# Softcapped attention and two feed-forward layers on one core: the column maxima put into PSUM, fewer and longer TensorE runs for the attention pairs, and a new placing of the planned steps

## The chip, the cores and the metric

One core of one Trainium2 chip runs the whole kernel. The metric is device time in microseconds of one execution. The engines are TensorE (PE; its weight loads are listed apart as PEld), VectorE (DVE), ScalarE (ACT), GpSimd (POOL) and SyncE (SP), which here only issues DMAs.

## The reference, cut to what matters

```
# q, k, v: (4 batches, 12 heads, 448 positions, 64), float32
scores = q @ k^T / sqrt(64)
scores = cap * tanh(scores / cap)
attn   = exp(scores - max over keys);  attn /= sum over keys + 1e-9
x      = attn @ v                     # heads side by side: (1792, 768)
h      = relu(x @ w_in)               # 768 -> 2048
x      = (h * h) @ w_out              # 2048 -> 768
g, val = x @ w_gate, x @ w_val        # 768 -> 1536 each
out    = (g * sigmoid(g) * val) @ w_out2   # 1536 -> 768
```

All is float32. The feed-forward matrices and their inputs are split into a high and a low float32r part, and each product is made of three matmuls (high by high, high by low, low by high).

## The kernel before, in words

**Attention pairs.** Two heads of a batch make a pair; six pairs a batch, 24 in all, numbered n = 6b + p. A pair goes through: load of k and q (`load_kq`) and of v; transposition to kT (batches 0 and 1: on TensorE by `tr_pe`, then two ScalarE copies by `tr_copy`; batches 2 and 3: on VectorE by `tr_v`); four blocks of 112 keys by 2 x 448 queries, each `scores` (TensorE, tile sc) and `tanh` (ScalarE, PSUM to SBUF, tile te or tt); `top`, three VectorE maxima over the four blocks (tile mx); `reduce`, a partition maximum on GpSimd (L250, tile mr); `sub`, four VectorE subtractions of mr (L256); `exp`, four on ScalarE (L260). Batches 0 and 1 then take `row_sum` and `av` on TensorE for each block; batches 2 and 3 add the four blocks first on VectorE (`total`, tile sm), then `total_sum` makes the sums and `av` weighs v, into two halves of one PSUM tile. `recip` is four steps on VectorE (a transpose L315 out of PSUM; small scalar steps L319 and L322; a reciprocal L326; a transpose L329), then `norm` (L334) and the split of the result by `x_hi` (ScalarE) and `x_lo` (VectorE, L348).

**Feed-forward units.** Pass 0 takes batches 0 and 1 with each weight piece, pass 1 batch 2, pass 2 batch 3. A unit is one output block of 128 by 448: six or four steps of three matmuls (`unit_mm`, L453, tile ff). In pass 0 each weight piece is loaded and rebuilt by three VectorE integer steps (`w_decode`, L418, L420, L422), stored to DRAM for the later passes, and split by `w_hi` (ScalarE) and `w_lo` (VectorE, L442). What leaves PSUM goes through ScalarE (relu, square, tanh) and VectorE (L480, L484, L492, L500).

**Order.** Nothing is ordered by hand. `Plan.order` places steps one by one: of all that could start, the one with the earliest start by the durations given to `plan.add`, and among equals the lowest rank (the fourth argument). The engines' instruction streams are then fixed in that order. The twelve pairs of batches 0 and 1 come ahead of nearly all feed-forward work (this stretch is called the attention stretch here); the pairs of batches 2 and 3 are strewn into passes 0 and 1, each opened by a unit named in `gates`, spaced by FIRST and LAST. `NPRE` = 3 weight pieces are used for batch 0 first, then for batch 1.

**PSUM**, eight banks: one score tile of two banks (tag s), a second (tag a: odd score blocks early, sums and weighed v later), four single banks (tag f) for everything else.

Of the kernel before, what the change touches and what calls it, by code (L numbers as in the profile page):

```python
# [20 lines left out]
class Plan:  # L21
# [15 lines left out]
    def order(self, free):  # L37
# [15 lines left out]
        blocked = {}  # L53
        dma = 0.0
        while len(seq) < len(ops):
            best = None
            for eng, some in ready.items():
                first = None
                for i in some:
                    _, _, _, rank, _, _, _, alloc, _ = ops[i]  # L60
                    t = max(since[i], free[eng])
                    for tag, bufs, _ in alloc:
                        old = rings.get(tag, ())
                        if len(old) >= bufs:
                            for d in old[-bufs]:
# [13 lines left out]
            if eng == "SP":  # L79
                free["SP"] = t + dur[0]  # L80
                dma = max(dma, t + 1.1) + dur[1]
                end[key] = dma + 1.1
            else:
                free[eng] = end[key] = t + dur
            seq.append((t, i))
# [11 lines left out]
def kernel(  # L97
# [33 lines left out]
    GB, TBUF, NPRE, NWARM = 10, 4, 3, 30  # L131
    FIRST = [17.0, 16.0]
    LAST = [60.0, 35.0]
# [7 lines left out]
    ps_f = ctx.enter_context(tc.tile_pool(name="ps_f", bufs=4, space=PSUM))  # L141

    V, A, G, PE = nc.vector, nc.scalar, nc.gpsimd, nc.tensor
    plan = Plan()
# [23 lines left out]

    def load_kq(b, p):
        d = pair[b, p] = {}  # L170
        if b < EARLY:
            n = ap.tile([CP, 2, NC, 2, D], F32, tag="kq", bufs=2, name="kq")
            for i, src in enumerate((k, q)):
                if (b, p) == (0, 0):
                    for j in range(2):
                        nc.sync.dma_start(n[:, i, :, j], src[b, j].rearrange("(p c) d -> p c d", c=NC))
                else:
                    nc.sync.dma_start(n[:, i], src[b, 2 * p : 2 * p + 2].rearrange("j (p c) d -> p c j d", c=NC))
        else:
            n = ap.tile([P, 2, TB, 32], F32, tag="kq", bufs=2, name="kq")  # L180
            for i, src in enumerate((k, q)):
                for g in range(4):
                    j, e = divmod(g, 2)
                    nc.sync.dma_start(
# [11 lines left out]
    def tr_pe(b, p, i):  # L196
        d = pair[b, p]
        pt = d["tr", i] = ps_f.tile([P, 512], F32, tag="f", name="tr")
        for c in range(NC):
            col = slice(c * CP, (c + 1) * CP) if i == 0 else slice(c, S, NC)  # L200
            PE.matmul(
                pt[:, col],
# [13 lines left out]
    def tr_copy(b, p, i):  # L216
        A.copy(kt(b, p)[:, i], pair[b, p].pop(("tr", i))[:, :S])
# [4 lines left out]
    def scores(b, p, c, tag):  # L222
        d = pair[b, p]
        pool = ps_s if tag == "s" else ps_a
        ps = d["s", c] = pool.tile([P, 2, 512], F32, tag=tag, name="sc")
        for j in range(2):
            r = slice(64 * j, 64 * j + 64)
            PE.matmul(  # L228
                ps[:CP, j, :S], d["kT"][r, 0, c * CP : (c + 1) * CP], d["kT"][r, 1], start=True, stop=True
            )  # L230

    def tanh(b, p, c):
        d = pair[b, p]
        if b < EARLY and c < 3:
            t = fp.tile([CP, 2, S], F32, tag="g", bufs=GB, name="te")
        else:
            t = ap.tile([CP, 2, S], F32, tag="t", bufs=TBUF, name="tt")
        d["t", c] = t
        A.activation(t, d.pop(("s", c))[:CP, :, :S], AF.Tanh, scale=c_inv)  # L239
# [7 lines left out]
    def reduce(b, p):  # L247
        d = pair[b, p]
        d["m"] = ap.tile([CP, 2, S], F32, tag="m", bufs=2, name="mr")
# [13 lines left out]
    def row_sum(b, p, c):  # L263
        d = pair[b, p]
        if c == 0:
            d["rs"] = ps_f.tile([P, 512], F32, tag="f", name="rs")
# [17 lines left out]
    def total_sum(b, p):  # L284
        d = pair[b, p]
        d["a"] = ps_a.tile([P, 2, 512], F32, tag="a", name="av")
        d["rs"] = d["a"][:, 1]
# [10 lines left out]
    def av(b, p, c):  # L298
        d = pair[b, p]
        if c == 0:  # L300
            d["av"] = ps_f.tile([P, 512], F32, tag="f", name="av") if b < EARLY else d["a"][:, 0]
        for j in range(2):
# [6 lines left out]
            )  # L309

# [134 lines left out]

    def unit_mm(ps, i, b, c):
# [3 lines left out]
        if c == 0:  # L450
            ffn_ps[i, b] = ps_f.tile([P, 512], F32, tag="f", name="ff")
# [50 lines left out]
    def out_tr(b, m):  # L502
        if m % 2 == 0:
            ob_t[b, m // 2] = fp.tile([P, TB, 2, 32], F32, tag="ob", bufs=2, name="ob")
# [20 lines left out]
    ACT1, ACT2, DVE1, DVE2 = 0.5, 0.98, 0.58, 1.04  # L525

    def plan_pair(n, at, gate=()):
        b, p = divmod(n, KD)
        early = b < EARLY
        pe = 0.0 if early else 0.8  # L530
        K = lambda name, *a: (name, n, *a)
        before = [("ld", n - 1)] if n else []
        add(K("ld"), "SP", (2.0, 1.4) if n == 0 else (1.3, 2.0) if early else (3.2, 1.5), at, load_kq, (b, p),
            before + list(gate), [("kq", 2, [K("tr", 0), K("tr", 1)])])
        add(K("lv"), "SP", (0.5, 0.7), at + 4, load_v, (b, p), [K("ld")], [("v", 2, [K("av", 3)])])
        for i in range(2):
            if early:
                add(K("tr", i), "PE", 0.56, at + 6, tr_pe, (b, p, i), [K("ld"), ("ident",)], [("f", 4, [K("cp", i)])])
                add(K("cp", i), "ACT", ACT1, at + 6, tr_copy, (b, p, i), [K("tr", i)],
                    [("kT", 2, [K("sc", 3)])] if i == 0 else [])  # L540
            else:
                add(K("tr", i), "DVE", DVE1, at + 6, tr_v, (b, p, i), [K("ld")],
                    [("kT", 2, [K("sc", 3)])] if i == 0 else [])
        src = K("cp", 1) if early else K("tr", 1)
        for c in range(NC):
            tag = "a" if early and c % 2 else "s"
            deps = [src, K("cp" if early else "tr", 0)] + ([K("sc", c - 1)] if c else [])
            add(K("sc", c), "PE", 0.78, at + 8 + c, scores, (b, p, c, tag), deps, [(tag, 1, [K("th", c)])], pe)
            tt = ("g", GB) if early and c < 3 else ("t", TBUF)
            add(K("th", c), "ACT", ACT2, at + 8.5 + c, tanh, (b, p, c), [K("sc", c)] + [("cap",)] * (n == 0),  # L550
                [(*tt, [K("av", c), K("rs", c) if early else K("tot", max(c, 1))])])
            if c:
                add(K("top", c), "DVE", DVE2, at + 9 + c, top, (b, p, c), [K("th", c), K("th", c - 1)] + [K("top", c - 1)] * (c > 1),
                    [("mx", 2, [K("par")])] if c == 1 else [])
        add(K("par"), "POOL", 3.2, at + 13, reduce, (b, p), [K("top", 3)], [("m", 2, [K("sub", 3)])])
        for c in range(NC):
            add(K("sub", c), "DVE", DVE2, at + 16 + c, sub, (b, p, c), [K("par")] + [K("sub", c - 1)] * (c > 0))
            add(K("ex", c), "ACT", ACT2, at + 17 + c, exp, (b, p, c), [K("sub", c)])
            if early:
                add(K("rs", c), "PE", 0.42, at + 18 + c, row_sum, (b, p, c), [K("ex", c)] + [K("rs", c - 1)] * (c > 0),  # L560
                    [("f", 4, [K("rc", 0)])] if c == 0 else [])
            elif c:
                add(K("tot", c), "DVE", DVE2, at + 19 + c, total, (b, p, c), [K("ex", c), K("ex", c - 1)],
                    [("mx", 2, [K("rs")])] if c == 1 else [])
        if not early:
            add(K("rs"), "PE", 0.5, at + 23, total_sum, (b, p), [K("tot", 3)], [("a", 1, [K("norm")])], pe)
        for c in range(NC):
            deps = [K("ex", c), K("lv")] + [K("av", c - 1)] * (c > 0) + [K("rs")] * (not early)
            add(K("av", c), "PE", 0.78, at + 19 + c, av, (b, p, c), deps,
                [("f", 4, [K("norm")])] if early and c == 0 else [], pe)  # L570
        for i, dur in enumerate((0.36, 0.7, 0.2, 0.62)):
            ring = {0: [("st", 1, [K("rc", 1)])], 1: [("rc", 2, [K("rc", 3)])], 3: [("rb", 1, [K("norm")])]}
            add(K("rc", i), "DVE", dur, at + 24 + i, recip, (b, p, i),
                [K("rc", i - 1)] if i else [K("rs", 3) if early else K("rs")], ring.get(i, ()))
        rel = [K("hold")] if b == 2 else [K("xl")]
        add(K("norm"), "DVE", DVE1, at + 28, norm, (b, p), [K("rc", 3), K("av", 3)], [("xs", 2, rel)])
        if b == 2:
            add(K("hold"), "SP", (0.4, 0.6), at + 30, hold, (p,), [K("norm")])
        else:
            s = lambda: x_t[b, p]  # L580
            add(K("xh"), "ACT", ACT1, at + 29, x_hi, (b, p, s), [K("norm")])
            add(K("xl"), "DVE", DVE1, at + 30, x_lo, (b, p, s), [K("xh")])
# [3 lines left out]
    PAIR = 7.6  # L586
# [27 lines left out]
    add(("ident",), "POOL", 8.0, -99, lambda: None)  # L614
    add(("cap",), "DVE", 0.8, -99, set_cap, (), [])
    for n in range(EARLY * KD):
        plan_pair(n, 10.6 * n)
    for i in range(NWARM):
        add(("warm", i), "PE", 0.43 if i < 8 else 0.22, 1e4 + i, warm, (i,), [("warm", i - 1)] if i else [],
            [("f", 4, [("warm", NWARM - 1)])] if i == 0 else [])  # L620
# [3 lines left out]
    for ps, (bs, seq) in enumerate(passes):  # L624
        for i in range(NB):
# [4 lines left out]
            if ps == 0:  # L630
                at = max(at - 14.0, 30.0 + 20 * i) if i < NPRE else at - 14.0
# [19 lines left out]
    for ps, (bs, seq) in enumerate(passes):  # L651
# [10 lines left out]
        for ps_, i, b, t in [s for s in steps if s[0] == ps]:  # L662
# [4 lines left out]
            for c in range(n):  # L667
# [103 lines left out]
```

## Time and profile before

| | |
|---|---|
| median of 3 runs | 1293.4 us (1288.98 to 1297.14) |
| the profiled execution | 1293.31 us, span 1291.3 us |
| busy share | PE 97%, PEld 77%, DVE 70%, ACT 44%, POOL 6% |
| chain that ended last | PE 83%, DVE 13%, ACT 1%, issue 1% |
| partition maxima | 24 on POOL, 77.9 us |
| feed-forward matmuls | 4896, 1020.9 us busy |

The profiled execution stands 0.1 us from the median and lies 2.0 us above its own span. A share of the whole span is a mean over two unlike stretches: the attention stretch, which lasts until about 179 us, and the feed-forward passes behind it. They are to be read apart.

### The profile page before, as it was taken

What the parts mean: (1) busy time and instruction counts of PE and PEld (TensorE: products, weight loads), DVE (VectorE), ACT (ScalarE), POOL (GpSimd) and SP (SyncE); (2) the same over time, 40 slices, a digit from 0 to 9 for tenths busy, and PEclk for the clock granted to TensorE, in tenths of its full rate; (3) what the DMA queues carried; (4) which work ended last, traced back from release to release, by engine and by line L of the source; (5) the groups of instructions that cost most, each with busy time, mean ns of one, the idle gap of its engine ahead of it and who ended that gap; (6) DMA issues with size and microseconds to landing.
All of it is one profiled execution on the core that took longest, in us unless ns stands there. A gap on an engine that the chain in (4) does not pass through costs nothing.

```text
span 1291.3 us, 16640 instructions
## 1 busy us (share of the span) xinstructions
PE 1246.6 (97%) x6300; PEld 996.8 (77%) x6300; DVE 906.4 (70%) x1341; ACT 568.6 (44%) x847; POOL 78.7 (6%) x31
## 2 busy tenths in 40 slices
PE   9887989999999999999999999999999999999997
PEld 5232457987986987987988987787787799999997
DVE  5999977668667867678778665777856843455454
ACT  6676644425344324323133375553453455433331
POOL 2232200000000000000000010000000000000000
PEclk9898989999998999999999999999999999999999
DMA  8331134664562572672664844254143353343323
GB/s 181 70 80 37 43 90 127 191 166 135 166 175 87 179 186 72 204 190 79 206 172 112 217 122 119 66 132 131 49 127 93 85 149 110 95 126 102 107 90 75
DMA packets 221983, 159.55 MB, mean 124 GB/s; under 512 B 143184, under 2 KB 190416, under 8 KB 221904
## 3 DMA queue, kind: packets, MB, share of 16 engines
q1 hardware_dynamic: 221904, 158.50, 43.8%
q8 instruction: 49, 0.80, 0.3%
q14 instruction: 30, 0.25, 0.1%
HBM read 124.85 MB, written 33.62 MB: 123 GB/s over the span
## 4 chain that ended last, share of the span: by engine, by line
PE 83%; DVE 13%; issue 1%; ACT 1%; SPq 0%; DMA 0%; DVEq 0%; ACTq 0%
PE ff L453 73%; PE av L303 4%; PE sc L228 4%; DVE mx L245 3%; DVE te L256 2%; DVE tt L256 1%; DVE rc L322 1%; DVE rc L319 1%; DVE sm L282 1%; PE warm L521 1%; DVE st L315 1%; PE rs L269 1%; DVE rb L329 1%; DVE wp L442 1%; DVE x L348 0%
## 5 line engine op out<-in xcount | busy, mean ns | idle before, releaser
L453 PE MATMUL ff<-x,wp 128*128 128x448 f32 x2880 | 600.9, 368 | 0.2 <-DVE x L348 0.2
L453 PEld LDWEIGHTS ff<-x,wp 128*128 128x128 f32 x2880 | 538.6, 188 | 71.9 <-issue 25.7
L453 PE MATMUL ff<-g,wp 128*128 128x448 f32 x2016 | 420.0, 367 | 0.1
L453 PEld LDWEIGHTS ff<-g,wp 128*128 128x128 f32 x2016 | 376.4, 188 | 48.9 <-issue 15.1
L437 ACT CAST wp<-wx 128x512 fp32r<-128x512 f32 (+1 forms) x246 | 176.9, 723 | 204.2 <-PE ff L453 141.4
L442 DVE TENSOR_TENSOR wp<-wx,wp 128x512 fp32r<-128x512 f32 (+1 forms) x246 | 206.8, 843 | 52.5 <-ACT wp L437 47.7
L492 DVE TENSOR_TENSOR g<-gg,g 128x448 fp32r<-128x448 f32 x112 | 69.9, 626 | 101.1 <-ACT g L488 101.0
L250 POOL PARTITION_ALL_REDUCE mr<-mx x24 | 77.9, 3247 | 926.3 <-DVE mx L245 926.3
L500 DVE TENSOR_TENSOR acc<-ff,acc 128x448 f32<-128x448 f32 x120 | 74.2, 621 | 48.7 <-PE ff L453 48.1
L228 PE MATMUL sc<-kT 64*112 64x448 f32 x384 | 93.7, 580 | 12.7 <-ACT te L239 10.9
L488 ACT CAST g<-gg 128x448 fp32r<-128x448 f32 x112 | 63.3, 565 | 71.6 <-DVE gg L484 69.7
L239 ACT ACTIVATE tt<-sc,capt 112x896 f32<-112x896 f32 x60 | 60.5, 1008 | 57.5 <-PE sc L228 57.3
L468 ACT ACTIVATE r<-ff 128x448 f32<-128x448 f32 x64 | 34.8, 544 | 91.3 <-PE ff L453 91.3
L476 ACT ACTIVATE th<-ff 128x448 f32<-128x448 f32 x48 | 26.2, 545 | 100.6 <-PE ff L453 100.6
L422 DVE SCALAR_TENSOR_TENSOR wx<-wr,wx 128x512 int32<-128x512 int32 (+1 forms) x82 | 68.4, 834 | 1.5
L420 DVE SCALAR_TENSOR_TENSOR wx<-wr,wx 128x512 int32<-128x512 int32 (+1 forms) x82 | 67.2, 820 | 2.1
L480 DVE SCALAR_TENSOR_TENSOR sg<-th,ff 128x448 f32<-128x448 f32 x48 | 29.6, 620 | 53.5 <-ACT th L476 53.3
L228 PEld LDWEIGHTS sc<-kT 64*112 64x112 f32 x384 | 27.9, 173 | 49.8 <-issue 22.7
L260 ACT ACTIVATE tt<-tt,capt 112x896 f32<-112x896 f32 x60 | 60.0, 1038 | 10.3 <-DVE tt L256 10.3
L303 PE MATMUL av<-tt,v 112*64 112x448 f32 x240 | 55.6, 576 | 7.8 <-DVE st L315 7.8
L256 DVE TENSOR_TENSOR tt<-tt,mr 112x896 f32<-112x896 f32 x60 | 62.1, 1084 | 1.1 <-POOL mr L250 1.1
L484 DVE SCALAR_TENSOR_TENSOR gg<-ff,sg 128x448 f32<-128x448 f32 x48 | 29.9, 623 | 33.8 <-PE ff L453 33.7
(54 smaller groups left out, 668.2 us busy)
## 6 DMA issues: line engine op xcount, KB each, us to landing
wx<-w SPq DMA_DIRECT2D x80, 384.0 KB, 3.1
wx<-w SPq DMA_DIRECT2D x84, 256.0 KB, 2.6
w<-wx SPq DMA_DIRECT2D x40, 384.0 KB, 2.7
wr<-in_moe_w_in_dram SPq DMA_DIRECT2D x16, 768.0 KB, 5.5
wr<-in_moe_w_out_dram SPq DMA_DIRECT2D x24, 512.0 KB, 4.0
w<-wx SPq DMA_DIRECT2D x42, 256.0 KB, 2.3
wr<-in_moe_w_gate_dram SPq DMA_DIRECT2D x12, 768.0 KB, 4.9
wr<-in_moe_w_val_dram SPq DMA_DIRECT2D x12, 768.0 KB, 4.9
```

Of the source, the lines that this page charges most:

```text
L228: PE.matmul(ps[:CP, j, :S], d["kT"][r, 0, c * CP : (c + 1) * CP], d["kT"][r, 1], start=True, stop=True)
L250: G.partition_all_reduce(d["m"].rearrange("p j s -> p (j s)"), d["mx"].rearrange("p j s -> p (j s)"), CP, bass_isa.ReduceOp.max)
L256: V.tensor_tensor(d["t", c], d["t", c], d["m"], ALU.subtract)
L303: PE.matmul(d["av"][64 * j : 64 * j + 64, :S], d["v"][:, j, c], d["t", c][:, j], start=(c == 0), stop=(c == NC - 1),)
L420: V.scalar_tensor_tensor(x, hi, -0x40000000, x, ALU.bitwise_and, ALU.bitwise_or)
L422: V.scalar_tensor_tensor(x, lo, 29, x, ALU.logical_shift_right, ALU.bitwise_or)
L437: A.copy(hl[:, 0], raws[ps, i])
L442: V.tensor_tensor(hl[:, 1], raws[ps, i], f32(hl[:, 0]), ALU.subtract)
L453: PE.matmul(ffn_ps[i, b][:, :S], hl[:, h, c], x[:, t], start=(c == 0 and s == 0), stop=(c == cnt(u) - 1 and s == 2),)
L488: A.copy(g_t[b, f][:, 0], tmp_t[i, b])
L492: V.tensor_tensor(g[:, 1], tmp_t.pop((i, b)), f32(g[:, 0]), ALU.subtract)
L500: V.tensor_tensor(acc, pt, acc, ALU.add)
```

## The change

- **Maxima in PSUM, for the twelve early pairs.** A new ScalarE step `top_copy` (planned as `mp`) copies mr into a PSUM tile (tag a); the four `sub` read it there. mr has one buffer in place of two. Late pairs' `sub` still read mr in SBUF.
- **Steps beside a partition maximum.** The planner is given a set `ports` of VectorE step names (top, xl, yl, wd, wl, rc, tot, gl). One whose start would lie within a planned partition maximum is planned at its end. No wait is added to the program by that.
- **Early PSUM.** The four f banks become two f0 and two f1. Early odd score blocks go into two f0 banks, one for each head, each with a tanh of its own; both transposes of a pair share one s tile and one ScalarE copy; sums and weighed v take f1.
- **The first pair** is loaded as the late ones are, k on SyncE's queue and q on ScalarE's, and transposed on VectorE.
- **Late pairs.** Two score blocks are one TensorE step into s and a, so two runs in place of four; `weigh` makes sums and all of `av` in one step, sums in a, weighed v in s.
- **Batch 1 begun ahead.** The first three units of batch 1 no longer wait for all its x and for the unit before them: each of their six steps needs only the x of one pair, and they may start once the last early tanh is done, in banks f0, f0 and s.
- **Placing.** All ranks, the planner's durations, and FIRST and LAST are new; the first pieces' rebuilding has ranks behind the early pairs; a fourth weight buffer (WP); the output tiles ob share the mx buffers.

```
-    def __init__(self):
+    def __init__(self, ports):
...
+                    if ops[i][0][0] in self.ports and pool[0] <= t < pool[1]:
+                        t = pool[1]
...
+    FIRST = [18.4, 16.8]
+    LAST = [66.8, 51.7]
+    DECODE = 138.4
...
+    def top_copy(b, p):
+        d = pair[b, p]
+        ps = ps_a.tile([P, 2, 512], F32, tag="a", name="mp")[:CP, :, :S]
+        A.copy(ps, d["m"])
+        d["m"] = ps
...
+    def weigh(b, p):
+        total_sum(b, p)
+        for c in range(NC):
+            av(b, p, c)
...
+        if halves(b, c):
+            ps = [ps_f.tile([P, 512], F32, tag="f0", name="sc")[:CP, :S] for _ in range(2)]
...
+                add(K("sc", c), "PE", 1.55, R("sc", c), lambda b, p, c: (scores(b, p, c), scores(b, p, c + 1)), (b, p, c),
+                    src + ([K("sc", c - 2)] if c else []), [("s", 1, [K("th", c)]), ("a", 1, [K("th", c + 1)])], pe)
...
+        if early:
+            add(K("mp"), "ACT", ACT2, R("mp"), top_copy, (b, p), [K("par")], [("a", 1, [K("sub", 3)])])
...
+                ahead = ps == 0 and b == 1 and i < NPRE
+                if c == 0 and u[0] == "1a" and not ahead:
...
+                if ahead and c == 0:
+                    deps.append((("th", EARLY * KD - 1, 3, 1), ("sub", EARLY * KD - 1, 3))[i == 3])
```

## Rows read from the trace of the kernel before

**Rows 1.** Busy time by windows: per engine us (instructions), then PEclk, DMA share, GB/s.
```profile
120.00:140.00 20.00, 17.50 (x131) 7.52 (x129) 19.37 (x31) 14.16 (x20) 2.86 (x1) 1.00 0.09 24
400.00:410.00 10.00, 7.31 (x26) 2.31 (x27) 7.69 (x17) 1.63 (x4) 0.00 (x0) 0.66 0.14 44
1100.00:1200.00 100.00, 100.00 (x496) 92.68 (x495) 52.88 (x76) 37.90 (x62) 0.00 (x0) 1.00 0.35 105
```

**Rows 2.** Groups of VectorE by form, 0 to 176 us.
```profile
L256 DVE TENSOR_TENSOR te<-te,mr 112x896 f32<-112x896 f32 x36 | 39.0, 1117 | 0.0
L322 DVE TENSOR_SCALAR rc<-st 32x7 f32<-32x7 f32 x46 | 15.3, 333 | 0.9
...
L319 DVE TENSOR_SCALAR rc<-st 128x14 f32<-128x14 f32 x12 | 9.8, 819 | 0.4
```

**Rows 3.** Timeline of VectorE in the attention stretch, and its last split.
```profile
14.96 1.09 DVE L245 TENSOR_TENSOR mx<-te 112x896 f32<-112x896 f32 x1 [10.77 <-ACT te L239]
...
19.50 2.57 DVE L245 TENSOR_TENSOR mx<-te 112x896 f32<-112x896 f32 x1
...
113.48 2.57 DVE L256 TENSOR_TENSOR te<-te,mr 112x896 f32<-112x896 f32 x1
...
116.41 0.17 DVE L319 TENSOR_SCALAR rc<-st 128x14 f32<-128x14 f32 x1
116.61 0.69 DVE L322 TENSOR_SCALAR rc<-st 32x7 f32<-32x7 f32 x4
...
178.82 0.61 DVE L348 TENSOR_TENSOR x<-xs,x 128x448 fp32r<-128x448 f32 x1
```

**Rows 4.** Timeline of GpSimd: one of the twelve early partition maxima, and a late one.
```profile
112.86 3.42 POOL L250 PARTITION_ALL_REDUCE mr<-mx  x1 [1.13 <-DVE mx L245]
...
815.15 2.86 POOL L250 PARTITION_ALL_REDUCE mr<-mx  x1 [44.73 <-DVE mx L245]
```

**Rows 5.** Timeline of VectorE beside the late one.
```profile
815.47 0.63 DVE L500 TENSOR_TENSOR acc<-ff,acc 128x448 f32<-128x448 f32 x1 [0.49 <-PE ff L453]
816.34 1.30 DVE L442 TENSOR_TENSOR wp<-wx,wp 128x768 fp32r<-128x768 f32 x1 [0.24 <-ACT wp L437]
```

**Rows 6.** Groups of ScalarE by form, 0 to 176 us.
```profile
L239 ACT ACTIVATE te<-sc,capt 112x896 f32<-112x896 f32 x36 | 34.9, 999 | 11.3 <-PE sc L228 11.2
```

**Rows 7.** Timeline of TensorE, attention stretch and just behind it.
```profile
10.33 1.70 PE L201 MATMUL tr<-ident,kq 112*128 112x112 f32 x16
...
131.80 1.76 PE L228 MATMUL sc<-kT 64*112 64x448 f32 x8
133.50 0.99 PE L201 MATMUL tr<-ident,kq 112*128 112x112 f32 x8
...
179.49 8.11 PE L453 MATMUL ff<-x,wp 128*128 128x448 f32 x38 [0.21 <-DVE x L348]
```

**Rows 8.** Chain of waits, one of the twelve late pairs: start, length, what.
```profile
219.98 69.01 PE ff L453 x333
288.99 0.94 PE sc L228 x4
289.93 2.01 PE ff L453 x9
...
314.80 0.52 PE av L290 x8
315.32 0.93 PE av L303 x4
...
316.83 2.48 PE av L303 x12
```

**Rows 9.** Waits of TensorE, 176 to 1291 us: total, times, longest.
```profile
PE av L303 <- DVE st L315: 7.8, 12, 1.1
PE av L290 <- DVE sm L282: 3.8, 2, 2.6
PE sc L228 <- DVE kT L220: 1.7, 1, 1.7
```

More of the change, by code (lines that the diff above doesn't have):

```diff
@@ L130 @@
     EARLY = 2
-    GB, TBUF, NPRE, NWARM = 10, 4, 3, 30
-    FIRST = [17.0, 16.0]
-    LAST = [60.0, 35.0]
+    GB, TBUF, WP, NPRE, NWARM = 10, 4, 4, 3, 30
+    FIRST = [18.4, 16.8]
+    LAST = [66.8, 51.7]
+    STRETCH = 2.91
+    AHEAD = dict(
+        ld=29.0, lv=13.4, tr=4.9, cp=4.1, sc=8.7, th=-4.3, top=-8.2, par=-0.6, mp=5.4, sub=29.5,
+        ex=22.2, rs=-1.8, av=30.4, rc=15.3, norm=-7.2, xh=27.4, xl=40.7,
+    )
+    LATER = dict(
+        ld=-14.4, lv=-4.9, tr=6.7, sc=-5.8, th=7.5, top=4.5, par=11.1, sub=28.9, ex=17.9,
+        tot=26.9, av=13.2, rc=1.5, norm=-0.6, xh=24.3, xl=36.9,
+    )
+    PACE = 6.97
+    SLACK = 2.11
+    MARGIN = 0.61
+    DECODE = 138.4
     const = ctx.enter_context(tc.tile_pool(name="const", bufs=1))
@@ L167, with rows @@
     x_t = {}
+    def rows(b, p):
+        return 0 < b * KD + p < EARLY * KD
     def load_kq(b, p):
         d = pair[b, p] = {}
-        if b < EARLY:
+        if rows(b, p):
             n = ap.tile([CP, 2, NC, 2, D], F32, tag="kq", bufs=2, name="kq")
             for i, src in enumerate((k, q)):
[L174 to L178, printed above, removed]
+                nc.sync.dma_start(n[:, i], src[b, 2 * p : 2 * p + 2].rearrange("j (p c) d -> p c j d", c=NC))
         else:
@@ L197, in tr_pe @@
         d = pair[b, p]
-        pt = d["tr", i] = ps_f.tile([P, 512], F32, tag="f", name="tr")
+        if i == 0:
+            d["tr"] = ps_s.tile([P, 2, 512], F32, tag="s", name="tr")
         for c in range(NC):
@@ L214, in kt, with tr_copy, halves, scores @@
         return d["kT"]
-    def tr_copy(b, p, i):
-        A.copy(kt(b, p)[:, i], pair[b, p].pop(("tr", i))[:, :S])
+    def tr_copy(b, p):
+        A.copy(kt(b, p), pair[b, p].pop("tr")[:, :, :S])
     def tr_v(b, p, i):
         V.transpose(out=kt(b, p)[:, i], in_=pair[b, p]["n"][:, i].rearrange("p t d -> p (t d)"))
-    def scores(b, p, c, tag):
+    def halves(b, c):
+        return b < EARLY and c % 2
+    def scores(b, p, c):
         d = pair[b, p]
-        pool = ps_s if tag == "s" else ps_a
-        ps = d["s", c] = pool.tile([P, 2, 512], F32, tag=tag, name="sc")
+        if halves(b, c):
+            ps = [ps_f.tile([P, 512], F32, tag="f0", name="sc")[:CP, :S] for _ in range(2)]
+        elif c % 2:
+            ps = ps_a.tile([P, 2, 512], F32, tag="a", name="sc")[:CP, :, :S]
+        else:
+            ps = ps_s.tile([P, 2, 512], F32, tag="s", name="sc")[:CP, :, :S]
+        d["s", c] = ps
         for j in range(2):
             r = slice(64 * j, 64 * j + 64)
[L228 to L232, printed above, removed]
+            to = ps[j] if halves(b, c) else ps[:, j]
+            PE.matmul(to, d["kT"][r, 0, c * CP : (c + 1) * CP], d["kT"][r, 1], start=True, stop=True)
+    def tanh(b, p, c, j=0):
         d = pair[b, p]
-        if b < EARLY and c < 3:
-            t = fp.tile([CP, 2, S], F32, tag="g", bufs=GB, name="te")
-        else:
-            t = ap.tile([CP, 2, S], F32, tag="t", bufs=TBUF, name="tt")
-        d["t", c] = t
-        A.activation(t, d.pop(("s", c))[:CP, :, :S], AF.Tanh, scale=c_inv)
+        if j == 0:
+            if b < EARLY and c < 3:
+                t = fp.tile([CP, 2, S], F32, tag="g", bufs=GB, name="te")
+            else:
+                t = ap.tile([CP, 2, S], F32, tag="t", bufs=TBUF, name="tt")
+            d["t", c] = t
+        if halves(b, c):
+            A.activation(d["t", c][:, j], d["s", c][j], AF.Tanh, scale=c_inv)
+        else:
+            A.activation(d["t", c], d.pop(("s", c)), AF.Tanh, scale=c_inv)
     def top(b, p, c):
@@ L248, in reduce @@
         d = pair[b, p]
-        d["m"] = ap.tile([CP, 2, S], F32, tag="m", bufs=2, name="mr")
+        d["m"] = ap.tile([CP, 2, S], F32, tag="m", name="mr")
         G.partition_all_reduce(
@@ L265, in row_sum @@
         if c == 0:
-            d["rs"] = ps_f.tile([P, 512], F32, tag="f", name="rs")
+            d["rs"] = ps_f.tile([P, 512], F32, tag="f1", name="rs")
         for g in range(4):
@@ L285, in total_sum @@
         d = pair[b, p]
-        d["a"] = ps_a.tile([P, 2, 512], F32, tag="a", name="av")
-        d["rs"] = d["a"][:, 1]
+        d["rs"] = ps_a.tile([P, 2, 512], F32, tag="a", name="rs")[:, 0]
         for g in range(4):
@@ L300, in av @@
         if c == 0:
-            d["av"] = ps_f.tile([P, 512], F32, tag="f", name="av") if b < EARLY else d["a"][:, 0]
+            if b < EARLY:
+                d["av"] = ps_f.tile([P, 512], F32, tag="f1", name="av")
+            else:
+                d["av"] = ps_s.tile([P, 2, 512], F32, tag="s", name="av")[:, 0]
         for j in range(2):
@@ L450, in unit_mm @@
         if c == 0:
-            ffn_ps[i, b] = ps_f.tile([P, 512], F32, tag="f", name="ff")
+            tag = f_tag(ps, i, b)
+            if tag in "sa":
+                ffn_ps[i, b] = (ps_s if tag == "s" else ps_a).tile([P, 2, 512], F32, tag=tag, name="ff")[:, 0]
+            else:
+                ffn_ps[i, b] = ps_f.tile([P, 512], F32, tag=tag, name="ff")
         for s, (h, t) in enumerate(((0, 0), (0, 1), (1, 0))):
@@ L555, in plan_pair @@
[L555 to L558, printed above, removed]
+        add(K("lv"), "SP", (0.5, 0.7), R("lv"), load_v, (b, p), [K("ld")], [("v", 2, [K("av", 3) if early else K("av")])])
+        tk = ("kT", 2, [K("sc", 3) if early else K("sc", 2)])
@@ new lines, in plan_pair @@
+        if rows(b, p):
+            for i in range(2):
+                add(K("tr", i), "PE", 0.42, R("tr"), tr_pe, (b, p, i), [K("ld"), ("ident",)] + [K("tr", 0)] * i + [("sc", n - 2, 3)] * (n > 1),
+                    [] if i else [("s", 1, [K("cp")])])
+            add(K("cp"), "ACT", ACT2, R("cp"), tr_copy, (b, p), [K("tr", 1)], [tk])
+            src = [K("cp")]
+        else:
+            for i in range(2):
+                add(K("tr", i), "DVE", 0.64, R("tr"), tr_v, (b, p, i), [K("ld")] + [K("tr", 0)] * i, [] if i else [tk])
+            src = [K("tr", 0), K("tr", 1)]
@@ new lines, in plan_pair @@
+        for c in range(NC):
+            half = halves(b, c)
+            ths = [K("th", c, 0), K("th", c, 1)] if half else [K("th", c)]
+            if early:
+                deps = src + ([K("sc", c - 1)] if c else [])
+                if c == 0 and n:
+                    deps.append(("sc", n - 1, 3))
+                add(K("sc", c), "PE", 0.84, R("sc", c), scores, (b, p, c), deps,
+                    [("f0", 2, [t]) for t in ths] if half else [("s", 1, ths)])
+            elif c % 2 == 0:
+                add(K("sc", c), "PE", 1.55, R("sc", c), lambda b, p, c: (scores(b, p, c), scores(b, p, c + 1)), (b, p, c),
+                    src + ([K("sc", c - 2)] if c else []), [("s", 1, [K("th", c)]), ("a", 1, [K("th", c + 1)])], pe)
+            tt = ("g", GB) if early and c < 3 else ("t", TBUF)
+            used = [K("av", c), K("rs", c)] if early else [K("av"), K("tot", max(c, 1))]
+            by = K("sc", c) if early else K("sc", c - c % 2)
+            for j, t in enumerate(ths):
+                add(t, "ACT", 0.51 if half else ACT2, R("th", c + 0.5 * j), tanh, (b, p, c, j),
+                    [by] + [("cap",)] * (n == 0) + ([ths[0]] if j else []), [] if j else [(*tt, used)])
+            if c:
+                prev = [K("th", 0)] if c == 1 else [K("top", c - 1)]
+                add(K("top", c), "DVE", DVE2, R("top", c), top, (b, p, c), ths + prev, [("mx", 2, [K("par")])] if c == 1 else [])
@@ L562, in plan_pair @@
             elif c:
-                add(K("tot", c), "DVE", DVE2, at + 19 + c, total, (b, p, c), [K("ex", c), K("ex", c - 1)],
-                    [("mx", 2, [K("rs")])] if c == 1 else [])
+                add(K("tot", c), "DVE", DVE2, R("tot", c), total, (b, p, c), [K("ex", c), K("ex", c - 1)],
+                    [("mx", 2, [K("av")])] if c == 1 else [])
         if not early:
[L566 to L570, printed above, removed]
@@ L586 @@
-    PAIR = 7.6
+            add(K("xh"), "ACT", ACT1, R("xh"), x_hi, (b, p, s), [K("norm")])
+            add(K("xl"), "DVE", DVE1, R("xl"), x_lo, (b, p, s), [K("xh")])
+    PAIR = 6.64
     steps = []
```

109 lines of the change are left out of this document (53 added, 56 removed).

## Prediction

> **What bounds the kernel now.** I read the windows first, because the page's shares mix two stretches. Up to about 179 us VectorE is the full engine: 19.37 of 20 us busy between 120 and 140, with TensorE at 17.50 and ScalarE at 14.16; in the feed-forward part it is TensorE, 100.00 of 100, with VectorE at 52.88 [rows 1]. So a microsecond taken from VectorE is worth something in the first stretch only, and one taken from TensorE in the second.
>
> The second view is VectorE's timeline. Its work starts in earnest at 14.96 and the last split of the attention stretch ends at 178.82 + 0.61 = 179.43 [rows 3]: 164.5 us, almost without idle time. But busy is not the same as working. The first step of `recip` (L319) takes 0.17 us when it starts behind the partition maximum, the four steps of L322 together 0.69 [rows 3], yet their means are 0.819 and 0.333 each [rows 2]. The excess is 12 x (0.819 - 0.17) = 7.8 us and 46 x (0.333 - 0.172) = 7.4 us. Four larger steps, the first at 19.50 and the last at 113.48, also have 2.3 to 2.6 us where a subtraction has 1.1 [rows 2, 3]: some 5.7 us together. Laid beside GpSimd's timeline, the step at 113.48 begins 0.6 us after a maximum does (112.86, 3.42 us) [rows 3, 4]. So about 21 us of VectorE's "busy" time is waiting beside twelve partition maxima, 1.7 us for each.
>
> The third view, the chain of waits, gives the price of a late pair on TensorE: four score runs of 0.94 us, each followed by nine feed-forward matmuls that take 2.01 where 69.01 / 333 x 9 = 1.87 would do, then sums 0.52, 0.93 for the first block of av, a hole, and 2.48 for the rest [rows 8]. The waits name the hole: the transpose L315 that reads the sums, 7.8 us over 12 pairs [rows 9].
>
> **The attention stretch.** Removing 21 us of collisions needs two things: the `sub` steps must not collide, and they must be what stands beside a maximum. For the first, the nearest rows are late ones. Beside the maximum at 815.15, L500, which reads one operand from PSUM, starts 0.32 us into it and takes 0.63; L442, with both operands in SBUF, starts 0.87 us later and takes 1.30 [rows 4, 5]; its 768 columns should take 0.95, an estimate between 0.61 for 448 columns and 1.09 for 896 [rows 3]. One row is thin, so I keep both ends: no gain from PSUM operands, or all of it. I take nearly all. [...] Four `sub` of 1.1 us are 4.4 us, longer than a maximum of 2.9 to 3.5 us [rows 2, 4], so a pair's `sub` can cover the next pair's maximum. But the engines' orders are fixed and nothing waits: a maximum that starts later or earlier than planned meets other steps again, and where no `sub` is ready VectorE idles instead. I take 17 of 21 us, with 21 and 6 as the ends.
>
> [...]
>
> What is added does not lie on VectorE. `top_copy` is one ScalarE step of some 1.0 us a pair by the tanh of the same size [rows 6]; halved odd tanhs add two starts a pair, some 0.2 us if a start costs there what 0.61 for 448 columns beside 1.09 for 896 shows on VectorE [rows 3]; one transposition copy in place of two gives 0.1 back. At 164.5 / 12 = 13.7 us a pair, ScalarE's 14.16 of 20 [rows 1] is 9.7 us a pair; it becomes 10.8, under the 12.3 that I expect VectorE to take. Without that slack the 13 us would lie on the path. The copy also lengthens the way from a maximum to its `sub` by 1.0 us and a handover, covered by the next pair's maxima and `recip` on VectorE. One buffer for mr is enough, as the copy empties it.
>
> **The start.** The first transposes on TensorE start at 10.33, then come a copy and the scores, and VectorE's first maximum is at 14.96 [rows 3, 7]. With kT made on VectorE, the scores can stand where the transposes stood, 1.6 us earlier; the warming matmuls ahead of them stay. Four DMA issues move to ScalarE's queue, which idles then. I take -1.5 (0 to -3).
>
> Together the stretch would end at 179.4 - 17 - 1.5 = 161. As a check, 164.5 us less the collisions is 143 us of VectorE work; from 13.4 that is 156 with no idle time, so my value leaves 5 us of idle time.
>
> **Batch 1 begun ahead.** After 179.49 TensorE does 38 matmuls of these three units in 8.11 us [rows 7]. In the new order nine must wait for the last split (three units, one step), 9 x 0.207 = 1.9 us. That is 6 us, if TensorE has room earlier (2.5 us free in 20 [rows 1], and the collisions' end takes some) and if the next weight piece is rebuilt in time, which is VectorE work that now ranks behind the pairs. I take -4, from -6 to 0.
>
> **Late pairs.** Two blocks in one run take 1.70 us (131.80 to 133.50) [rows 7] in place of 2 x 0.94: 0.36 a pair. Two fewer returns to feed-forward matmuls save 2 x (2.01 - 1.87) = 0.28. Sums and weighed v in tiles of their own remove the hole, 319.31 - 314.80 - (0.52 + 0.93 + 2.48) = 0.58 [rows 8]. That is 1.22 us a pair, 14.7 us for twelve, on an engine with nothing to hide it. The new run needs both score tiles free; behind a run stand feed-forward matmuls, so what is late is tanh on ScalarE, not TensorE. I take -14.5 (-10 to -15).
>
> **Stalls in passes 0 and 1.** [...] The larger planned slack ahead of the late TensorE steps helps; closer spacing (LAST 66.8 and 51.7) puts more VectorE work between units. I take -4, between -9 and +3. The output tiles in the mx buffers cost nothing, as no pair is under way when they are written; the fourth weight buffer and the new PSUM tags leave the feed-forward rotation as it was.
>
> **Sum.** -17 - 1.5 - 4 - 14.5 - 4 = -41, against 1293.3: 1252 us.
>
> **Rivals.** *Everything falls into place*: -21 - 3 - 6 - 15 - 9 = -54, 1239 us. [...] Against: it needs VectorE full for 143 us behind a chain of four engines.
>
> *The collisions stay*: PSUM operands are not spared, or `sub` and maximum do not meet in time, or VectorE idles where it waited before. The stretch then gives 6, batch 1 ahead 2, and the rest stands: -6 - 1 - 2 - 14 - 2 = -25, 1268. For it: the thin row, and that the planner adds no wait. This is also the case in which the change does not do what it says.
>
> *TensorE paces the attention stretch at its lower level*: with VectorE freed, TensorE (17.50 of 20 [rows 1]) is next; holes that drop its granted clock would cost it several microseconds. This lies between forecast and the last case, 1258 to 1268.
>
> *The single tile s paces it* (slower): transposes and both even score blocks of a pair must now pass one buffer: 0.99 + 1.0 + 2 x (0.94 + 1.0) = 5.9 us [rows 6 to 8], with six handovers of some 0.2 [rows 7] about 7. Each handover also waits for whatever its engine has in hand. If that were 2 us each time, the cycle would be 19 us against 164.5 / 12 = 13.7 now, the stretch would grow by 64, the other parts would give 24 back, and the time would be about 1333. It decides against the change from 13.7 + 24 / 12 = 15.7 us a pair on. Against it: pieces in hand are mostly of 1 us, and the cycle then stays at 13.
>
> **How the numbers follow.** Forecast 0.50, everything 0.20, collisions or clock 0.22, no change to speak of 0.04, slower 0.04. One per cent, 13 us, is about what three runs that spread over 8 us can tell from no change. Faster by over 1%: 0.91; within: 0.05; slower: 0.04. The range from 1236 to 1274 takes in both neighbouring cases and leaves out little over 1 in 10.
>
> **What would show it.** Right: L319 and L322 near 0.17 each throughout; `sub` near 1.1 us beside maxima; last split near 161; four score runs become two of 1.7; no wait of av on L315. Wrong: VectorE with idle time in the attention stretch ended by ScalarE or TensorE (the s tile, or `top_copy`); long L319 as before; TensorE idle just behind the last split, waiting for a weight piece; new waits of late runs for tanh.

## The result, and the profile after

The changed kernel takes 1242.13 us (median of 4, 1239.81 to 1242.57) against 1292.74 for the kernel before: ratio 0.9604, 95% interval 0.9571 to 0.9637, 50.6 us. The profiled execution has a span of 1240.4 us, 50.9 less than before.

**Attention stretch.** Busy time by windows, to be laid beside [rows 1]:

```profile
120.00:140.00 20.00, 20.00 (x138) 8.07 (x137) 17.42 (x32) 17.38 (x24) 4.20 (x2) 1.00 0.05 13
140.00:160.00 20.00, 20.00 (x141) 9.54 (x139) 18.02 (x34) 12.59 (x16) 3.17 (x1) 1.00 0.28 59
400.00:410.00 10.00, 10.00 (x51) 9.27 (x50) 9.85 (x14) 3.45 (x6) 0.00 (x0) 1.00 0.60 199
1100.00:1200.00 100.00, 100.00 (x495) 92.69 (x494) 49.84 (x70) 37.31 (x61) 0.00 (x0) 1.00 0.33 103
```

The full engine between 120 and 160 us is now TensorE, no longer VectorE; the hole near 400 is gone. VectorE's groups by form, answering to [rows 2]:

```profile
L296 DVE TENSOR_TENSOR te<-te,mp 112x896 f32<-112x896 f32 x36 | 37.5, 1080 | 1.2 <-ACT mp L291 1.2
...
L369 DVE TENSOR_SCALAR rc<-st 32x7 f32<-32x7 f32 x48 | 7.8, 162 | 0.9
...
L366 DVE TENSOR_SCALAR rc<-st 128x14 f32<-128x14 f32 x12 | 2.1, 173 | 0.3
```

The small steps are at 0.17 and 0.16 us each and the subtractions at 1.08: no collision shows any longer. VectorE's timeline, answering to [rows 3]: first maximum, three subtractions, last split.

```profile
10.73 1.09 DVE L278 TENSOR_TENSOR mx<-te 112x896 f32<-112x896 f32 x1 [3.20 <-ACT te L270]
...
106.21 3.08 DVE L296 TENSOR_TENSOR te<-te,mp 112x896 f32<-112x896 f32 x3
...
165.58 0.62 DVE L395 TENSOR_TENSOR x<-xs,x 128x448 fp32r<-128x448 f32 x1
```

And GpSimd's timeline, answering to [rows 4]:

```profile
105.98 3.04 POOL L283 PARTITION_ALL_REDUCE mr<-mx  x1 [8.35 <-ACT mp L291]
```

Three subtractions run beside that maximum at full pace; the third ends at 109.29, 0.27 us behind it. The stretch ends at 166.20, 13.2 us earlier than 179.43.

**Late pairs.** The chain of waits, one pair, to be laid beside [rows 8]:

```profile
213.21 52.89 PE ff L510 x255
266.10 1.69 PE sc L259 x8
267.79 3.24 PE ff L510 x15
...
303.92 0.52 PE rs L329 x8
304.44 3.16 PE av L345 x16
307.59 48.84 PE ff L510 x240
```

Two score runs of 1.69; sums and av in 0.52 + 3.16 = 3.68 where 4.51 stood, with no hole. The view of TensorE's waits behind 166 us, which named 13.3 us before [rows 9], names none.

**Where the 50.9 us came from.** 13.2 ahead of the last split and 37.7 behind it (1111.9 before, 1074.2 now). Behind it: sums and av 12 x 0.83 = 10.0; scores 12 x (4 x 0.94 - 2 x 1.69 + 0.28) = 7.9; waits other than the hole 3.8 + 1.7 = 5.5; 19 feed-forward matmuls fewer (4826, now 4807), 3.9. Some 10 remain. Part of them is TensorE at a lower granted clock in the kernel before, which fell after idle time of 1.7 us near 189 and of 2.6 us near 400. Its chain of waits there:

```profile
190.28 3.34 PE ff L453 x9
...
402.08 0.88 PE av L290 x8
402.96 1.72 PE av L303 x4
...
405.26 4.34 PE av L303 x12
```

Nine matmuls took 3.34 us in place of 2.02 (clock 0.66 between 190 and 195), and one pair's sums and av took 6.94 in place of 0.52 + 0.93 + 2.48 (0.59 between 405 and 410). With two score runs near 190 that is 4.6 us. In the changed kernel the granted clock is 1.00 from 166.2 to 1230. The other 5 to 6 us are in the feed-forward matmuls' own pace; the last section tells what is known of it. TensorE's groups behind the last split, before and after (the other 2016 feed-forward matmuls are the same number in both):

```profile
L453 PE MATMUL ff<-x,wp 128*128 128x448 f32 x2810 | 585.4, 368 | 0.2 <-DVE x L348 0.2
```

```profile
L510 PE MATMUL ff<-x,wp 128*128 128x448 f32 x2791 | 575.8, 366 | 0.0
```

### The profile page after: what moved, and what is told of

Read it like the earlier page. It is cut to its first block, busy times and chain, and to the rows that moved or that the text cites. A ratio compares the mean times of both kernels' runs of the same rounds, so it can differ in the third digit from the quotient of the medians.

```text
span 1240.4 us, 16621 instructions
## 1 busy us (share of the span) xinstructions
PE 1221.9 (99%) x6292; PEld 998.4 (80%) x6292; DVE 877.5 (71%) x1343; ACT 578.4 (47%) x870; POOL 72.4 (6%) x31
## 4 chain that ended last, share of the span: by engine, by line
PE 93%; DVE 3%; ACT 1%; issue 1%; DMA 0%; POOL 0%; DVEq 0%; ACTq 0%
PE ff L510 81%; PE av L345 5%; PE sc L259 5%; PE rs L309 1%; DVE mx L278 1%; DVE te L296 1%; PE rs L329 0%; ACT tt L270 0%; ACT te L300 0%; DMA kq<-in_q_dram 0%; DVE tt L296 0%; POOL mr L283 0%; ACT mp L291 0%; DVE rb L376 0%; DMA kq<-in_k_dram 0%
## 5 line engine op out<-in xcount | busy, mean ns | idle before, releaser
L510 PE MATMUL ff<-g,wp 128*128 128x448 f32 x2016 | 415.3, 366 | 0.0
L484 ACT CAST wp<-wx 128x768 fp32r<-128x768 f32 (+1 forms) x246 | 175.9, 723 | 198.8 <-PE ff L510 148.4
L489 DVE TENSOR_TENSOR wp<-wx,wp 128x768 fp32r<-128x768 f32 (+1 forms) x246 | 199.9, 818 | 42.4 <-ACT wp L484 39.7
L283 POOL PARTITION_ALL_REDUCE mr<-mx x24 | 71.6, 2984 | 864.2 <-DVE mx L278 818.7
L259 PE MATMUL sc<-kT 64*112 64x448 f32 x384 | 90.5, 576 | 0.8 <-ACT te L272 0.4
L272 ACT ACTIVATE tt<-sc,capt 112x896 f32<-112x896 f32 x48 | 46.0, 1006 | 29.0 <-PE sc L259 29.0
L555 ACT COPY acc<-ff 128x448 f32<-128x448 f32 x48 | 25.6, 533 | 58.2 <-PE ff L510 58.2
L296 DVE TENSOR_TENSOR tt<-tt,mr 112x896 f32<-112x896 f32 x48 | 51.3, 1085 | 0.0
```

The lines of the kernel that those rows point to most:

```text
L259: PE.matmul(to, d["kT"][r, 0, c * CP : (c + 1) * CP], d["kT"][r, 1], start=True, stop=True)
L283: G.partition_all_reduce(d["m"].rearrange("p j s -> p (j s)"), d["mx"].rearrange("p j s -> p (j s)"), CP, bass_isa.ReduceOp.max)
L296: V.tensor_tensor(d["t", c], d["t", c], d["m"], ALU.subtract)
L484: A.copy(hl[:, 0], raws[ps, i])
L489: V.tensor_tensor(hl[:, 1], raws[ps, i], f32(hl[:, 0]), ALU.subtract)
L510: PE.matmul(ffn_ps[i, b][:, :S], hl[:, h, c], x[:, t], start=(c == 0 and s == 0), stop=(c == cnt(u) - 1 and s == 2),)
```

## The experiments

Each row's ratio is to the kernel before on the same chip. The kernel before had medians from 1291.7 to 1292.7 us beside all these runs, so differences between rows of about 1 us say nothing. The start of the first pair, the fourth weight buffer and the new ranks were not run apart.

| run | median us | ratio (95%) |
|---|---|---|
| a1 subtractions read SBUF | 1250.06 | 0.9686 (0.9659 to 0.9712) |
| a2 no port rule | 1250.77 | 0.9687 (0.9662 to 0.9711) |
| a3 batch 1 not ahead | 1243.22 | 0.9628 (0.9605 to 0.9652) |
| a4 four score steps | 1241.60 | 0.9606 (0.9569 to 0.9644) |
| a5 one late tile | 1241.47 | 0.9616 (0.9592 to 0.9640) |
| a6 old FIRST, LAST | 1248.65 | 0.9654 (0.9618 to 0.9690) |
| b1 before + late pairs new | 1269.24 | 0.9815 (0.9790 to 0.9840) |
| b2 before + two late tiles | 1278.68 | 0.9893 (0.9863 to 0.9923) |
| c1 quarter of the early sums | 1232.89 | 0.9539 (0.9513 to 0.9566) |
| c2 before + the same | 1290.36 | 0.9992 (0.9973 to 1.0011) |
| d1 pairs 8 to 11 transposed on VectorE | 1250.34 | 0.9663 (0.9631 to 0.9695) |
| d2 d1 and a3 | 1252.95 | 0.9684 (0.9654 to 0.9713) |

**a1: the operand alone.**

```
-        d["m"] = ap.tile([CP, 2, S], F32, tag="m", name="mr")
+        d["m"] = ap.tile([CP, 2, S], F32, tag="m", bufs=2, name="mr")
...
-        d["m"] = ps
+        d["mp"] = ps
```

> The changed kernel with every engine's order kept to the instruction; top_copy still runs, but the 48 early subtractions read mr in SBUF (two buffers). Theory (a VectorE step with both operands in SBUF cannot run beside the reading part of a partition maximum): subtractions that start 0.3 to 1.5 us into a maximum take 2.2 to 2.6 us in place of 1.08, some 1.2 to 1.5 us for each of nearly twelve maxima, 12 to 17 us on VectorE; part of it is taken up by the 17 us in which VectorE now idles, so the last split comes 8 to 14 us later and the time is 1250 to 1257. Rival (only which steps stand beside a maximum matters, the place of the operand does not): subtractions stay at 1.08 and the time at 1242 +- 2.

Every instruction stands where it stood; only where 48 steps read one operand differs. The groups of the first three blocks and of the fourth, then VectorE's timeline of one collision and of the last split:

```profile
L296 DVE TENSOR_TENSOR te<-te,mr 112x896 f32<-112x896 f32 x36 | 51.1, 1456 | 0.0
...
L296 DVE TENSOR_TENSOR tt<-tt,mr 112x896 f32<-112x896 f32 x12 | 13.0, 1080 | 0.0
...
57.68 4.57 DVE L296 TENSOR_TENSOR te<-te,mr 112x896 f32<-112x896 f32 x3
...
173.37 0.62 DVE L395 TENSOR_TENSOR x<-xs,x 128x448 fp32r<-128x448 f32 x1
```

GpSimd's timeline there:

```profile
57.32 3.17 POOL L283 PARTITION_ALL_REDUCE mr<-mx  x1 [8.19 <-DVE mx L278]
```

Beside that maximum three subtractions take 4.57 us in place of 3.08. Over all, 36 x (1.456 - 1.080) = 13.5 us of waiting returns; the last split comes at 173.99, 7.8 us later, and the time is 7.9 us above the changed kernel's. Behind the last split both kernels take the same 1074.2 us. So the operand's place is what frees the subtraction, and nearly half of the wait disappears in idle time that VectorE has anyway. That it is the reading part of a maximum that holds a step up was not shown by itself. The rival falls.

**a2: the planner's rule alone.**

```
-    plan = Plan({"top", "xl", "yl", "wd", "wl", "rc", "tot", "gl"})
+    plan = Plan(set())
```

> The changed kernel with an empty set of port steps, so the planner may put any step beside a maximum; the subtractions still read PSUM. Theory (the planner's rule is needed as well as the PSUM operand): L366 and L369 or other steps are stretched again beside most maxima, 5 to 15 us on VectorE, time 1246 to 1256. Rival (the ranks alone already lay the subtractions beside the maxima): nearly the same order, no long L366, 1240 to 1245.

VectorE's timeline, a collision and the last split:

```profile
108.17 2.05 DVE L467 SCALAR_TENSOR_TENSOR wx<-wr,wx 128x512 int32<-128x512 int32 x1
...
175.19 0.62 DVE L395 TENSOR_TENSOR x<-xs,x 128x448 fp32r<-128x448 f32 x1 [0.63 <-ACT x L391]
```

and GpSimd's:

```profile
107.89 2.97 POOL L283 PARTITION_ALL_REDUCE mr<-mx  x1 [8.39 <-ACT mp L291]
```

A weight step takes 2.05 us beside a maximum (0.69 elsewhere), the last split is 9.6 us later, and the time 8.6 us longer. What collides is weight steps and two `top` steps, hardly `recip`: a miss in the detail. The stretched steps are some 6 us longer in all, by their means against the changed kernel's; as the whole order was planned anew, the rest of the 8.6 us need not be collisions. Both halves are needed, each worth some 8 us with the other in place.

**c1 and c2: which engine paces the attention stretch.** Both leave out the row sums of three of the four blocks:

```
     def row_sum(b, p, c):
...
+        if c < NC - 1:
+            return
...
-                start=(c == 0),
-                stop=(c == NC - 1),
+                start=True,
+                stop=True,
```

> The changed kernel with the early pairs' row sums taken from the last of the four blocks alone, so early rows are divided by about a quarter of their sum: 12 x 3 x 0.52 = 18.7 us less TensorE work in the attention stretch, nothing less on VectorE. Theory (with the collisions gone TensorE paces the second half of that stretch): the last split comes 8 to 16 us earlier and the time is 1226 to 1234. Rival (VectorE still paces it, TensorE's full windows are only pipelining): 1 to 4 us earlier, 1238 to 1241.

> The same edit in the kernel before: row sums of the early pairs from the last block alone, 18.7 us less TensorE work up to 179 us. Theory (VectorE paces the stretch there): the last split within 3 us of 179.4, time 1289 to 1293. Rival (TensorE paced it already, collisions or not): 8 to 16 us earlier, 1277 to 1285.

The last splits, on VectorE's timelines; the changed kernel so edited:

```profile
156.19 0.62 DVE L397 TENSOR_TENSOR x<-xs,x 128x448 fp32r<-128x448 f32 x1
```

and the kernel before:

```profile
176.17 0.62 DVE L350 TENSOR_TENSOR x<-xs,x 128x448 fp32r<-128x448 f32 x1
```

The windows of the changed kernel so edited:

```profile
120.00:140.00 20.00, 19.38 (x101) 9.61 (x100) 19.40 (x39) 19.99 (x28) 6.03 (x2) 1.00 0.10 27
```

18.7 us less on TensorE (an estimate from 0.52 us for one block's sums) bring 9.4 us in the changed kernel (156.81 for 166.20; 9.2 us in the time) and 2.6 in the kernel before, where the ratio's interval takes in no change. So TensorE has become the pace of the stretch, and was not before. Only half comes out; VectorE and ScalarE are then full in their turn (19.40 and 19.99 of 20).

**a3: batch 1 ahead.**

```
-                ahead = ps == 0 and b == 1 and i < NPRE
+                ahead = False
...
-        if ps == 0 and b == 1 and i < NPRE:
-            return ("f0", "f0", "s", "a")[i]
```

> The changed kernel without the early start of batch 1's first three units: they wait for all x of batch 1 and for the unit before them, in the ordinary banks. Theory (TensorE has idle time in the attention stretch that these matmuls fill): 38 or more feed-forward matmuls of batch 1 stand behind the last split in place of 18 or so fewer, 4 to 6 us: 1246 to 1249. Rival (what follows is bound by the next weight pieces on VectorE, so the early start is waited away): 1242 +- 2.

Last split on VectorE's timeline:

```profile
160.45 0.61 DVE L395 TENSOR_TENSOR x<-xs,x 128x448 fp32r<-128x448 f32 x1
```

It comes at 161.06, 5.1 us earlier, 19 more matmuls stand behind it (2810, as in the kernel before, for 2791), and the part behind it is 3.6 us longer. The time is 1.1 us above the changed kernel's with intervals that overlap: the number is the rival's. But the matmuls begun ahead are not waited away afterwards, as the rival had it: they hold up the attention stretch by about what they save behind it, because TensorE paces both sides. My theory falls too.

**b1, b2, a5, a4: the late pairs.** b1 and b2 in the kernel before, a5 and a4 in the changed one. b2:

```
-        d["a"] = ps_a.tile([P, 2, 512], F32, tag="a", name="av")
-        d["rs"] = d["a"][:, 1]
+        d["rs"] = ps_a.tile([P, 2, 512], F32, tag="a", name="rs")[:, 0]
```

and av into a tile of s. b1 has this and, of the change, the two-block score step and sums and av in one step, with the old ranks:

```
+            elif c % 2 == 0:
+                add(K("sc", c), "PE", 1.55, at + 8 + c, lambda b, p, c: (scores(b, p, c, "s"), scores(b, p, c + 1, "a")), (b, p, c),
...
+            add(K("av", 0), "PE", 3.7, at + 23, lambda b, p: (total_sum(b, p), [av(b, p, c) for c in range(NC)]), (b, p), [K("tot", 3), K("lv")],
```

a5:

```
-        d["rs"] = ps_a.tile([P, 2, 512], F32, tag="a", name="rs")[:, 0]
+        d["a"] = ps_a.tile([P, 2, 512], F32, tag="a", name="rs"); d["rs"] = d["a"][:, 1]
...
-                d["av"] = ps_s.tile([P, 2, 512], F32, tag="s", name="av")[:, 0]
+                d["av"] = d["a"][:, 0]
```

a4:

```
-            elif c % 2 == 0:
-                add(K("sc", c), "PE", 1.55, R("sc", c), lambda b, p, c: (scores(b, p, c), scores(b, p, c + 1)), (b, p, c),
+            else:
+                add(K("sc", c), "PE", 0.78, R("sc", c), scores, (b, p, c),
```

> The kernel before with the late pairs alone as in the change: score blocks two by two into tiles s and a, sums and weighed v in one step and in tiles of their own; the early pairs' code, the ranks and the gates are those of before. Theory (a late pair's cost lies on TensorE, and these two edits alone shorten it by some 1.2 to 1.5 us): score runs 1.69, sums and av 0.52 and 3.16 with no hole, 15 to 18 us: 1274 to 1279. Rival (the runs are shorter but the pairs then wait for tanh or for totals, because the planner's slack was not raised): 1283 to 1293, with waits of TensorE behind 179 us well above 13 us.

> The kernel before with every engine's order kept; only the late pairs' sums and weighed v go into tiles of their own (a and s). Theory after the run of the changed kernel in one tile, which had no hole: the hole needs both the shared tile and the transpose emitted between the blocks of av, so two tiles alone also remove it: 12 x 0.58 = 7 us, 1285 to 1287. Rival (the hole is TensorE waiting for something else that ends at the same moment): no change, 1292 +- 3.

> The changed kernel with its order kept; only the late pairs' sums and weighed v share one PSUM tile again (two banks of it). Theory (the hole of 0.6 us in each late pair is TensorE waiting for the transpose that reads the sums, because both lie in one tile): the hole is back in 12 pairs, 0.58 to 0.65 us each, and the run of 3.16 us splits into 0.93 and 2.48, so 10 to 11 us in all: 1249 to 1253. Rival (the gain of the late pairs came from the one run of sums and av, in which nothing of feed-forward stands between): no hole, 1242 +- 2.

> The changed kernel with the late pairs' scores in four runs of one block again, blocks in tiles s and a by turns; sums and av stay in one step. Theory (a run of one block costs 0.94 and a return to feed-forward matmuls some 0.1 to 0.14 us): 12 x 2 x (0.19 + 0.10) to 12 x 2 x (0.19 + 0.14) = 7 to 8 us, 1249 to 1250. Rival (in the kernel before the four runs cost more than that because they also waited for the single tile s; with two tiles they are nearly free): 1242 to 1245.

The chain of waits of b2, at the same pairs as [rows 8]:

```profile
217.45 67.68 PE ff L452 x333
...
310.95 0.52 PE rs L289 x8
311.47 3.16 PE av L302 x16
```

of a5:

```profile
304.67 0.52 PE rs L329 x8
305.18 3.16 PE rs L345 x16
```

of a4, the first pair:

```profile
170.18 1.69 PE sc L259 x8
171.87 2.62 PE ff L510 x12
174.49 0.94 PE sc L259 x4
175.43 0.81 PE ff L510 x3
176.24 0.94 PE sc L259 x4
```

In the kernel before, two tiles alone close the hole. In the changed kernel one tile does not open it: `weigh` issues all of av before the transpose exists in the program, so nothing in the tile has to wait for it. The hole needed both the shared tile and the old order of issue, and either edit removes it (the new order with a shared tile was run only in the changed kernel, by a5). a4 shows the same of the scores: asked for single blocks, the planner still lays them side by side in 20 of the 24 runs, since two tiles are free (the second half of this first pair is one of the exceptions), and the time stays. Neither expectation for a5 or a4 as my theory gave it was met. b2 is worth 13.1 us, more than its 7, and b1 22.5, more than the 15 to 18: sums and av fall from 4.51 to 3.68 us, as 16 matmuls in one run take 3.16 where 4 and 12 took 0.93 + 2.48, which is 10.0 us for twelve pairs. In b2's profiled execution the clock also stays at 1.00 between 190 and 195, where it was 0.66 before, and 333 feed-forward matmuls behind a pair run faster (last section).

**a6: the places of the late pairs.**

```
-    FIRST = [18.4, 16.8]
-    LAST = [66.8, 51.7]
+    FIRST = [17.0, 16.0]
+    LAST = [60.0, 35.0]
```

> The changed kernel with FIRST and LAST of the kernel before, so the late pairs open where they did. Theory (the stalls behind the attention stretch went with the closer spacing and an earlier end of the pairs): waits of TensorE behind the last split come back, 3 to 6 us, 1245 to 1248. Rival (they went because runs are planned later after their inputs and are fewer; the places do not matter): 1242 +- 2, with no waits of TensorE.

TensorE's waits, 166 us to the end:

```profile
PE rs L329 <- DVE sm L322: 6.7, 1, 6.7
```

One pair's totals come 6.7 us late and the time is 6.5 us longer, so the places matter. A single wait carries it, but the likeness of the two numbers is chance. The granted clock falls to 0.50 between 985 and 990, after the wait, and sums and av of that pair take 2.8 us more than elsewhere; the last split, on the other hand, comes 2.6 us earlier (163.62). Of that pair, on TensorE's timeline:

```profile
986.79 5.69 PE L345 MATMUL av<-tt,v 112*64 112x448 f32 x16
```

**d1 and d2: less work on TensorE.** In d1:

```
-        return 0 < b * KD + p < EARLY * KD
+        return 0 < b * KD + p < 8
```

with k and q on SyncE's queue and the longer load in the plan for pairs 8 to 11; d2 has a3's edit besides.

> The changed kernel with the early pairs 8 to 11 loaded and transposed as the late ones are (VectorE, in place of TensorE and a ScalarE copy), loads on SyncE's queue: TensorE 4 x 0.9 = 3.6 us less in the second half of the attention stretch, ScalarE 4 us less, VectorE 4 x 1.2 = 5 us more. Theory (TensorE paces that half, VectorE has some 2 us free in 20): last split 1 to 4 us earlier, 1238 to 1241. Rival (VectorE is close enough to full that the swap costs it what it gives): 1242 to 1246.

> d1 without the early start of batch 1's units, so TensorE has 3.6 + 4 us less ahead of the last split and 4 us more behind it. Theory (work moved across the last split is neutral while TensorE paces both sides, so only the transpositions count): last split 5 to 8 us earlier, time as d1, 1238 to 1242. Rival (with VectorE pacing now, the feed-forward matmuls would have been free ahead of the split): 3 to 5 us above d1.

d1's chain of waits, two small steps of `recip`:

```profile
136.95 1.57 DVE rc L369
138.54 1.18 DVE rc L369
```

and its windows:

```profile
140.00:160.00 20.00, 13.81 (x90) 5.85 (x91) 18.17 (x34) 10.16 (x12) 0.00 (x0) 0.77 0.23 72
```

The maximum on GpSimd's timeline, and the feed-forward matmuls behind the last split in d1 and in d2:

```profile
136.82 2.86 POOL L283 PARTITION_ALL_REDUCE mr<-mx  x1 [4.62 <-DVE rc L366]
```

```profile
L510 PE MATMUL ff<-x,wp 128*128 128x448 f32 x2820 | 582.0, 366 | 0.0
```

```profile
L508 PE MATMUL ff<-x,wp 128*128 128x448 f32 x2825 | 582.4, 366 | 0.0
```

d1's time is 8.2 us above the changed kernel's, outside both ranges. In the new order `recip` meets a maximum again (1.57 and 1.18 us for 0.16), TensorE has holes, and its granted clock falls to 0.77. The last split comes at 170.31, 4.1 us later, and 29 more feed-forward matmuls (2820 for 2791) stand behind it, some 6 us: batch 1 is hardly ahead any longer. The rival's sign is right but not its reason alone. That the new order, planned without real waits, is what goes wrong is how I read it; no run shows it by itself. d2 is 2.6 us above d1 with intervals that overlap: with five matmuls more behind the split than d1, it took next to nothing away, and decides nothing.

## Why the prediction was right, point by point

- **Collisions.** They were what I took them for, and both halves of the edit are shown (a1: subtractions of 1.456 us for 1.080; a2: a weight step of 2.05 for 0.69). All of the 21 us left VectorE, where I took 17. The operand in PSUM costs the subtraction nothing that shows: it takes 1.080 us, and so does the fourth block's in a1, with both operands in SBUF.
- **End of the attention stretch: over-sized.** Forecast 161, measured 166.2, though the start gave 4.2 us (10.73 for 14.96) where I took 1.5. Without batch 1 ahead it ends at 161.06 (a3), and that this meets the forecast is luck: the collisions and the start together gave 25 us where I took 18.5, and some 7 of them did not come out. The rival in which TensorE paces the stretch came true between 120 and 160 without the lower clock there (20.00 of 20 at 1.00; c1 and c2 show the pace), but not its time of 1258 to 1268. The one tile s did not pace it: TensorE is never idle there between 120 and 160.
- **Batch 1 ahead: the step that failed.** I gave it 4 us "if TensorE has room earlier". It has none once VectorE is freed: the matmuls save 3.6 us behind the split and cost 5.1 ahead of it (a3), and the time shows no gain.
- **Late pairs: under-sized.** 14.5 us forecast; the runs and the hole measure 10.0 + 7.9 = 17.9 in the chain, and b1 22.5 in time. The scores were right (0.64 a pair forecast, 0.66 measured); sums and av were 0.83, not 0.58, because joining the blocks of av also shortens them. That new tiles remove the hole holds in the kernel before (b2) and is not what does it in the changed one (a5).
- **Stalls: under-sized.** I took 4, with 9 as the far end of the range, and no run shows that 9; what the runs showed in its place are named waits of 3.8 + 1.7 = 5.5 us and 4.6 us more on TensorE where the granted clock was 0.66 near 190 and 0.59 to 0.72 near 400. Both are gone in the changed kernel, whose clock is 1.00 there. a6 shows that they hang on the places: with the old ones TensorE waits 6.7 us.
- **Sum.** 41 us forecast, 50.6 measured. In the attention stretch I forecast 5 us too many, which is what batch 1 ahead cost there. Behind it I forecast 15 too few: 3.4 for the late pairs, 6 for the stalls, and 5 to 6 for the matmuls' own pace, a term that I did not have and whose cause is open. The time lies nearer to the rival in which everything falls into place (1239) than to the forecast (1252), but not by its terms: the stretch gave 13 us of its 24, the late pairs more than its 15.

## What to carry to other kernels

Busy time of VectorE next to GpSimd work is to be checked by the mean of a small step against its shortest: here 21 us of waiting were booked as work, and one operand in PSUM let the subtractions run through (1.080 us on the mean, 1.456 in a1, with both operands in SBUF). Once an engine is relieved, read the next one's windows before crediting work that is moved onto it: TensorE had 2.5 us free in 20 before and none after (between 120 and 140), and the work put there came back as a later end of the stretch (5.1 us, a3). The wait inside a tile hung here on the order of issue as much as on the tile, and either edit removed it (b2 and a5 both show 0.52 and 3.16 us with no hole between).

## What the runs showed that I had not expected

The same feed-forward matmuls run at two paces at a granted clock of 1.00, which holds through the stretches named here of the kernel before and of the changed one. In the kernel before, 333 of them behind a pair take 69.01 us, 0.2072 each [rows 8]; in b2, whose order is the same, 67.68, 0.2032. In the changed kernel 255 behind one pair take 52.89 (0.2074) and 240 behind the next 48.84 (0.2035). In b2, only banks and waits of the late pairs differ. It is 1.0 to 1.3 us for each such stretch; the cause was not found.
